# Chunked attention with a top-128 feed-forward: keys in runs of 16 tokens, V without zero blocks, casts off GpSimd, ranks summed on TensorE, a fixed issue order

## The chip, the cores and the metric

The kernel runs on one core of a Trainium2 chip. The core has five engines with a queue each: TensorE (PE in the profile, with its weight loads as PEld), VectorE (DVE), ScalarE (ACT), GpSimd (POOL) and SyncE (SP, which here only issues transfers). The metric is the device time of one execution in microseconds; the time before is the median of three runs, 202.14 us.

## The reference

The first half is attention in chunks. There are 4 batches, 8 heads, 768 tokens and 64 dimensions a head. Each chunk of 32 queries sees 8 memory keys, up to 16 tokens to the left of the chunk, the chunk itself and up to 8 tokens to its right:

```python
for c in range(nc):
    c_start, c_end = c * 32, c * 32 + 32
    l_start, r_end = max(0, c_start - 16), min(S, c_end + 8)
    k_full = concatenate([mem_k, k[:, :, l_start:r_end]]);  v_full = likewise
    scores = matmul(q_c, k_full.T) / 8
    a = softmax(scores)
    out[:, :, c_start:c_end] = matmul(a, v_full)
```

The second half takes the result as x of 4 x 768 rows of 512 columns and sends the best 128 rows of each batch through a feed-forward:

```python
scores = x @ w_gate
out = x.copy()
for b in range(B):
    top_idx = the 128 rows of batch b with the highest scores
    ye = maximum(x[b, top_idx] @ w1, 0) @ w2          # 512 -> 1024 -> 512
    out[b, top_idx] = x[b, top_idx] + sigmoid(scores)[:, None] * ye
```

## The kernel before

**Attention by pairs of heads.** Two heads form a pair (n), and a batch has four, so there are 16 pairs. Inside a pair, partitions 0 to 63 belong to the first head and 64 to 127 to the second. Three chunks form a group of 96 queries, and a pair has eight groups. A group's three chunks share one window of 120 tokens, which together with the 8 memory keys makes 128 keys. They are stored as 64 partitions with two tokens each: token 2i and 2i+1 lie on partition i (index s is the token's parity), and the memory keys sit on partitions 60 to 63. A mask per partition and chunk (`maskb`) blanks the keys that a chunk does not see; it is the bias of the exponential.

**What is done for a pair.** `tr_q` and `tr_k` transpose queries and keys on TensorE, 16 transposes of 96x64 each, both into the same PSUM tile (tag `tp`, one buffer). ScalarE copies the queries out (L205); VectorE copies the keys out with three copies (L217 for the six inner groups, L219 and L221 for the first and last) into `kw`, which holds the 128 keys of each group; GpSimd adds the memory keys (L223). `cast_v` turns V to 16 bits on GpSimd, two casts of 64 partitions (L230), into `vbd`, which is block diagonal: each head's 64 values and a column of ones have their own columns, and the other head's columns are zero, written once at the start (L160, L161). `scores(u)` does half a pair (u runs over 32 halves): 32 matmuls of 64x64 by 96 columns (L245) into two PSUM banks and three exponentials of 256 elements (L251). `values(u)` does 12 matmuls of 128 partitions by 130 columns, six on 96 queries (L266) and six on 32 (L270), and on VectorE a reciprocal and a product (L274, L275) that write the finished half into `x`.

**Loading.** q and k come through GpSimd's queue and are cast to 16 bits on the way (L77). V comes through SP's queue as 32 bits, in `load_v`: for each head one transfer for the inner groups (L86, 180 KB), one each for the first and last group (L88, L90) and one for the memory values (L93). `load_batch(b+1)` is coded at the second half of batch b; the V tiles have two buffers, and so have the tiles of q and k.

**The feed-forward of a batch** is spread over the eight halves of the next batch by `moe_steps`: `m_store` writes x out through SP (L288, L289), `m_scores` takes the dot products with w_gate on VectorE (L298) and casts x to 16 bits on GpSimd (L300), `m_rows` spreads the scores over all partitions (transposes L308, copies L310), `m_rank` counts for every row how many rows score higher, with a compare that also sums (L325), `m_select` turns the counts into 128 slots, `m_gather` collects the rows by matmul with the one-hot matrix `sel`, `m_ffn1` and `m_ffn2` are the two layers, and the end is a scattered transfer that adds to `out` (L379). Every PSUM tile of this part is the one bank `pm`. The batch that comes last has nothing beside it. The x tiles have two buffers, and transfers to `out` wait for one another where they overlap: the store of a batch and the scatters before and after it.

**The order.** The loop at L409 gives the order in the code, but the framework's planner reorders the instructions of each engine by its own estimates and by when their inputs are due. It decides where the steps of the feed-forward stand among the attention of the next batch.

Of the kernel before, what the change touches and what calls it, by code (L numbers as in the profile page):

```python
# [26 lines left out]
def kernel(  # L27
# [24 lines left out]
    HD = S * D  # L52
    SLOTS = 4
# [3 lines left out]
    att = ctx.enter_context(tc.tile_pool(name="att", bufs=3))  # L57
# [4 lines left out]
    pxx = ctx.enter_context(tc.tile_pool(name="pxx", bufs=2, space=bass.MemoryType.PSUM))  # L62
    ptt = ctx.enter_context(tc.tile_pool(name="ptt", bufs=1, space=bass.MemoryType.PSUM))
    pmm = ctx.enter_context(tc.tile_pool(name="pmm", bufs=1, space=bass.MemoryType.PSUM))


    q16s, k16s, v32s = {}, {}, {}
    vbufs = [cst.tile([128, NP, NG, 128], FP, tag=f"v32_{i}", name=f"v32_{i}") for i in range(2)]

    def alloc_batch(b):  # L70
        q16s[b] = ld.tile([96, H, 512], F16, tag="q16", name=f"q16_{b}")
        k16s[b] = ld.tile([96, H, 512], F16, tag="k16", name=f"k16_{b}")
        v32s[b] = vbufs[b % 2]
# [6 lines left out]
    def load_v(b, p0, n):  # L80
        t = v32s[b]
        for h in range(2):
            base = (b * H + 2 * p0 + h) * HD
            o = 64 * h
            for i in range(n):
                nc.sync.dma_start(out=t[o:o + 60, p0 + i, 1:7, :],  # L86
                                  in_=_dap(v, base + 2 * i * HD + 80 * D, [[2 * D, 60], [96 * D, 6], [1, 128]]))
            nc.sync.dma_start(out=t[o + 8:o + 60, p0:p0 + n, 0, :],  # L88
                              in_=_dap(v, base, [[2 * D, 52], [2 * HD, n], [1, 128]]))
            nc.sync.dma_start(out=t[o:o + 56, p0:p0 + n, 7, :],  # L90
                              in_=_dap(v, base + 656 * D, [[2 * D, 56], [2 * HD, n], [1, 128]]))
            for i in range(n):
                nc.sync.dma_start(out=t[o + 60:o + 64, p0 + i, :, :],  # L93
                                  in_=_dap(mem_v, (b * H + 2 * (p0 + i) + h) * n_mem * D,
                                           [[2 * D, 4], [0, NG], [1, 128]]))


    memk16 = cst.tile([n_mem, B * H, D], F16, tag="memk16")
    nc.gpsimd.dma_start(out=memk16, in_=_dap(mem_k, 0, [[D, n_mem], [n_mem * D, B * H], [1, D]]))
    alloc_batch(0)  # L100
    load_qk(0, q, q16s[0], 0, 1)
    load_qk(0, k, k16s[0], 0, 1)

    ident = cst.tile([128, 128], FP, tag="ident")
    make_identity(nc, ident)
    ident16 = cst.tile([128, 128], F16, tag="ident16")
    nc.vector.tensor_copy(out=ident16, in_=ident)

# [3 lines left out]
    load_v(0, 0, 1)  # L112
    load_qk(0, q, q16s[0], 1, 1)
    load_qk(0, k, k16s[0], 1, 1)
    load_v(0, 1, 1)
    load_qk(0, q, q16s[0], 2, 2)
    load_qk(0, k, k16s[0], 2, 2)
    load_v(0, 2, 2)

    wgb = cst.tile([128, Dm], FP, tag="wgb")  # L120
    nc.sync.dma_start(out=wgb, in_=_dap(moe_w_gate, 0, [[0, 128], [1, Dm]]))
    w1_sb = cst.tile([128, 4, F], F16, tag="w1")
    w2_sb = cst.tile([128, 8, Dm], F16, tag="w2")

# [5 lines left out]
    kp = cst.tile([128, 1], FP, tag="kp")  # L130
    for h in range(2):
        nc.gpsimd.iota(kp[64 * h:64 * h + 64, :], pattern=[[0, 1]], base=0, channel_multiplier=1,
                       allow_small_or_imprecise_dtypes=True)
    ismem = cst.tile([128, 1], FP, tag="ismem")
    nc.vector.tensor_scalar(out=ismem, in0=kp, scalar1=59.5, scalar2=None, op0=ALU.is_gt)
    maskb = cst.tile([128, 3], FP, tag="maskb")
    tmpm = cst.tile([128, 3], FP, tag="tmpm")
    for c in range(3):
        nc.vector.tensor_scalar(out=maskb[:, c:c + 1], in0=kp, scalar1=16.0 * c - 0.5, scalar2=None, op0=ALU.is_gt)
        nc.vector.tensor_scalar(out=tmpm[:, c:c + 1], in0=kp, scalar1=16.0 * c + 27.5, scalar2=None, op0=ALU.is_lt)  # L140
    nc.vector.tensor_tensor(out=maskb, in0=maskb, in1=tmpm, op=ALU.mult)
    nc.vector.tensor_tensor(out=maskb, in0=maskb, in1=ismem.to_broadcast([128, 3]), op=ALU.add)
    nc.vector.tensor_scalar(out=maskb, in0=maskb, scalar1=1.0, scalar2=-MASKED, op0=ALU.subtract, op1=ALU.mult)


    ones8 = cst.tile([128, NG], F16, tag="ones8")
    nc.vector.memset(ones8, 1.0)
    nc.vector.tensor_scalar(out=ones8[:, 0:1], in0=kp, scalar1=7.5, scalar2=None, op0=ALU.is_gt)
    nc.vector.tensor_scalar(out=tmpm[:, 0:1], in0=kp, scalar1=55.5, scalar2=None, op0=ALU.is_lt)
    nc.vector.tensor_tensor(out=ones8[:, 7:8], in0=tmpm[:, 0:1], in1=ismem, op=ALU.add)  # L150

    vbds, kws = [], []
    for i in range(SLOTS):
        vb = cst.tile([128, NG, 2, 130], F16, tag=f"vbd{i}", name=f"vbd{i}")
        kw = cst.tile([128, NG, 128], F16, tag=f"kw{i}", name=f"kw{i}")
        vbds.append(vb)
        kws.append(kw)
        nc.vector.memset(kw[:, 0, 0:16], 0.0)
        nc.vector.memset(kw[:, 7, 112:120], 0.0)
        nc.gpsimd.memset(vb[0:64, :, :, 65:130], 0.0)  # L160
        nc.gpsimd.memset(vb[64:128, :, :, 0:65], 0.0)  # L161
        for h in range(2):
            o = 64 * h
            nc.vector.tensor_copy(out=vb[o:o + 64, :, :, 65 * h + 64],
                                  in_=ones8[o:o + 64, :].unsqueeze(2).to_broadcast([64, NG, 2]))


    p_mk = ptt.tile([128, B * NP, n_mem], F16, tag="tp", name="p_mk")
    for pr in range(B * NP):
        nc.tensor.transpose(out=p_mk[:, pr, :], in_=memk16[:, 2 * pr:2 * pr + 2, :],  # L170
                            identity=ident16[0:n_mem, 0:n_mem])
    memkT = cst.tile([128, B * NP, n_mem], F16, tag="memkT")
    nc.vector.tensor_copy(out=memkT, in_=p_mk)


    iota1 = cst.tile([128, cap], F16, tag="iota1")
    nc.gpsimd.iota(iota1, pattern=[[1, cap]], base=1, channel_multiplier=0, allow_small_or_imprecise_dtypes=True)
    ltri = cst.tile([128, 128], F16, tag="ltri")
    nc.gpsimd.memset(ltri, 1.0)
    nc.gpsimd.affine_select(out=ltri, in_=ltri, pattern=[[1, 128]], compare_op=ALU.is_gt, fill=0.0,  # L180
                            base=0, channel_multiplier=-1)
    ones6 = cst.tile([128, NB], FP, tag="ones6")
    nc.vector.memset(ones6, 1.0)
    auxs = []
    for i in range(2):
        a = cst.tile([128, NB, 3], F16, tag=f"aux{i}", name=f"aux{i}")
        nc.gpsimd.iota(a[0:96, :, 0], pattern=[[96, NB]], base=0, channel_multiplier=1,
                       allow_small_or_imprecise_dtypes=True)
        nc.gpsimd.iota(a[96:128, :, 0], pattern=[[32, NB]], base=576, channel_multiplier=1,
                       allow_small_or_imprecise_dtypes=True)  # L190
        auxs.append(a)


    qTs = {}

# [204 lines left out]


    NPR = B * NP
    NU = 2 * NPR
    tr_q(0)
    tr_k(0)
    cast_v(0)
# [58 lines left out]
```

The softmax here doesn't subtract the row's maximum and nothing guards it: scores larger than these inputs give would overflow.

## Time and profile before

| | |
|---|---|
| median of 3 runs | 202.14 us (200.54 to 204.42) |
| the profiled execution | 200.01 us, its span 198.6 us |
| granted TensorE clock, mean over the span | 0.747 |
| busiest engines | PE 125.2 us, DVE 117.0 us, POOL 83.4 us |
| transfers | 24.49 MB in 29561 packets |
| V transfers issued by SP | 100 |
| last L275 of batches 1, 2 and 3 | 86, 126 and 168 us |

The profile's times run from the first instruction. L12 is line 12 of the kernel. A busy share is an average over stages that are limited by different things. An issue row of SP (SPq) gives the time in which SP handed out a transfer, not the time of the transfer. A windows row gives the busy time of each engine in that stretch with the number of instructions, then the granted clock (1.00 is full speed), the share of the 16 transfer engines that was busy, and GB/s.

### The profile page before, as it was taken

To read this page: it belongs to the slowest core of one execution; us is meant where nothing else is said; L and a number is where in the kernel's file an instruction comes from. 1 tells how busy PE (TensorE), PEld (TensorE's weight loads), DVE (VectorE), ACT (ScalarE), POOL (GpSimd) and SP (SyncE) were. 2 spreads that over 40 slices of the span, in tenths; PEclk is the share of its full clock that TensorE was granted. 3 is DMA by queue.
4 is the path that set the end of the run, shared out by engine and by line. 5 is a ranking of instruction groups with operands and counts; after the bars stand their busy time and mean duration, and the time that the engine had idled before them with its cause. 6 is when DMAs were issued, how large, how long until landed. Compare 5 with 4: busy or idle time off the path is not lost. (4 is left out here: it accounts for less than half of the span.)

```text
span 198.6 us, 4328 instructions
## 1 busy us (share of the span) xinstructions
PE 125.2 (63%) x1732; PEld 94.8 (48%) x1732; DVE 117.0 (59%) x309; ACT 62.6 (32%) x137; POOL 83.4 (42%) x104
## 2 busy tenths in 40 slices
PE   0313794958975499973685999567256994306550
PEld 0202673746645277842563787345155772105510
DVE  4284354342899921798998024999950459894010
ACT  2101552418544122654062317232102570200200
POOL 7999993034998000467404040679300004500020
PEclk9999998585995555896579559955558799555885
DMA  5997899999799999603987600049100000364003
GB/s 77 214 208 163 186 189 215 217 210 209 125 251 282 216 211 211 143 4 53 262 196 158 122 0 3 0 56 272 45 0 3 0 3 0 36 192 143 0 0 53
DMA packets 29561, 24.49 MB, mean 123 GB/s; under 512 B 2150, under 2 KB 25318, under 8 KB 29542
## 3 DMA queue, kind: packets, MB, share of 16 engines
q1 hardware_dynamic: 20438, 14.75, 30.1%
q0 software_dynamic: 9104, 9.47, 29.8%
q8 instruction: 13, 0.21, 0.5%
q14 instruction: 6, 0.05, 0.1%
HBM read 25.30 MB, written 7.34 MB: 164 GB/s over the span
## 5 line engine op out<-in xcount | busy, mean ns | idle before, releaser
L251 ACT ACTIVATE es<-p_s,maskb 128x256 f16<-128x256 f32 x96 | 37.8, 476 | 34.2 <-PE p_s L245 31.1
L230 POOL CAST vbd<-v 64x1024 f16<-64x1024 f32 x32 | 35.5, 1158 | 12.8 <-DMA v<-in_mem_v_dram 10.8
L300 POOL CAST x<-x 128x1536 f16<-128x1536 f32 x8 | 13.6, 1705 | 41.1 <-DVE x L275 41.1
L298 DVE SCALAR_TENSOR_TENSOR junk<-x,wgb 128x512 f32<-128x512 f32 x24 | 30.6, 1301 | 0.1
L245 PE MATMUL p_s<-qT,kw 64*64 64x96 f16 x512 | 23.9, 247 | 4.5 <-DVE kw L219 2.5
L217 DVE COPY kw<-p_tk 128x720 f16<-128x720 f16 x16 | 14.4, 902 | 19.2 <-PE p_tk L213 19.2
L245 PEld LDWEIGHTS <-kw 64*64 64x64 f16 x512 | 18.3, 137 | 12.5 <-issue 4.7
L325 DVE TENSOR_SCALAR_CACHE_REDUCE jr<-brow,scr 128x768 f16<-128x768 f32 x24 | 23.0, 1001 | 1.2 <-ACT brow L310 1.2
L205 ACT COPY qT<-p_tq 128x768 f16<-128x768 f16 x16 | 12.8, 803 | 33.3 <-PE p_tq L201 33.3
L201 PE MATMUL p_tq<-ident,q 96*64 96x96 f16 x256 | 14.2, 250 | 14.0 <-DVE kw L221 12.1
L266 PE MATMUL p_x<-vbd,es 128*96 128x130 f16 x192 | 21.2, 259 | 2.3 <-ACT es L251 0.9
L274 DVE RECIPROCAL rd<-p_x 128x6 f32<-128x6 f32 x32 | 6.0, 191 | 27.1 <-PE p_x L270 26.5
L270 PE MATMUL p_x<-vbd,es 128*32 128x130 f16 x192 | 19.9, 248 | 0.0
L266 PEld LDWEIGHTS <-es 128*96 128x96 f16 x192 | 16.4, 149 | 6.1 <-ACT es L251 2.4
L223 POOL COPY kw<-memkT 128x64 f16<-128x64 f16 x16 | 5.0, 317 | 32.9 <-PE p_s L245 32.4
L201 PEld LDWEIGHTS <-q 96*64 96x64 f16 x256 | 9.7, 135 | 17.5 <-issue 12.3
L275 DVE TENSOR_TENSOR x<-p_x,rd 128x384 f32<-128x384 f32 x32 | 17.5, 551 | 0.6
L308 PE MATMUL p_b<-ident,scr 128*128 128x128 f32 x24 | 8.2, 376 | 13.2 <-DVE junk L298 9.9
L213 PE MATMUL p_tk<-ident,k 96*64 96x96 f16 x256 | 12.9, 254 | 5.4 <-ACT qT L205 4.4
L270 PEld LDWEIGHTS <-es 128*32 128x32 f16 x192 | 12.9, 107 | 6.4 <-issue 3.0
L379 POOL DMA_INDIRECT out_dram<-y,idx x4 | 6.7, 1670 | 21.0 <-DVE y L378 20.5
L348 PE MATMUL p_e<-sel,x 128*128 128x128 f16 x96 | 13.3, 304 | 1.9 <-DVE sel L340 1.9
(70 smaller groups left out, 140.0 us busy)
## 6 DMA issues: line engine op xcount, KB each, us to landing
v<-in_v_dram SPq DMA_DIRECT2D x32, 180.0 KB
out_dram<-x SPq DMA_DIRECT2D x4, 1152.0 KB
q<-in_q_dram POOLq DMA_DIRECT2D x7, 384.0 KB, 9.6
k<-in_k_dram POOLq DMA_DIRECT2D x7, 384.0 KB, 11.8
w_sb<-in_moe_w_dram POOLq DMA_DIRECT2D x2, 1024.0 KB, 20.6
out_dram<-x SPq DMA_DIRECT2D x4, 384.0 KB
v<-in_v_dram SPq DMA_DIRECT2D x14, 56.0 KB
v<-in_v_dram SPq DMA_DIRECT2D x14, 52.0 KB
```

Of the source, the lines that this page charges most:

```text
L201: nc.tensor.transpose(out=p_t[64 * h:64 * h + 64, j, :], in_=q16s[b][:, 2 * pr + h, 64 * j:64 * j + 64], identity=ident16[0:96, 0:96])
L217: nc.vector.tensor_copy(out=kw[:, 1:7, 0:120].rearrange("p g (t j) -> p g t j", j=8), in_=_sap(p_t, 10, [[12, 6], [1, 15], [96, 8]]))
L230: nc.gpsimd.tensor_copy(out=vb[o:o + 64, :, :, 65 * h:65 * h + 64], in_=v32s[b][o:o + 64, pr, :, :].rearrange("p g (s d) -> p g s d", d=D))
L245: nc.tensor.matmul(out=p_s[o:o + 64, s, 96 * gi:96 * gi + 96], lhsT=kw[o:o + 64, g, s:128:2], rhs=qf[o:o + 64, 96 * g:96 * g + 96], start= ...
L251: nc.scalar.activation(out=es[:, :, :, 32 * c:32 * c + 32], in_=pv[:, :, :, 32 * c:32 * c + 32], func=AF.Exp, bias=maskb[:, c:c + 1], scal ...
L266: nc.tensor.matmul(out=p_x[0:96, gi, :], lhsT=es[:, s, gi, :], rhs=vb[:, GROUPS[half][gi], s, :], start=(s == 0), stop=(s == 1))
L270: nc.tensor.matmul(out=p_x[96:128, c, :], lhsT=es[:, s, 3, 32 * c:32 * c + 32], rhs=vb[:, GROUPS[half][3], s, :], start=(s == 0), stop=(s ...
L275: nc.vector.tensor_tensor(out=xs[b][:, 3 * half:3 * half + 3, 128 * pr:128 * pr + 128].rearrange("p g (h d) -> p g h d", d=D), in0=pv[:, : ...
L298: nc.vector.scalar_tensor_tensor(out=junk, in0=x[:, bl, :], scalar=1.0, in1=wgb, op0=ALU.mult, op1=ALU.mult, accum_out=m.scr[:, bl:bl + 1])
L300: nc.gpsimd.tensor_copy(out=m.x16[:, lo:hi, :], in_=x[:, lo:hi, :])
L325: nc.vector.tensor_scalar(out=jr, in0=m.brow, scalar1=m.scr[:, bl:bl + 1], scalar2=None, op0=ALU.is_gt, op1=ALU.add, accum_out=m.cnt[:, bl ...
L348: nc.tensor.matmul(out=p_e[:, dch, :], lhsT=m.x16[:, bl, 128 * dch:128 * dch + 128], rhs=m.sel[:, bl, :], start=(bl == 0), stop=(bl == NB ...
```

## The change

- V is loaded so that a partition holds a run: token t of a group's window goes to partition 16 j + i with t = 8 i + 2 j + s, so each head has four blocks (j) of 15 partitions, and the memory values sit on the 16th partition of each block. `load_v` issues each transfer once for each block.
- The keys follow the same order: two copies (one for each s) of 512 elements with 16 in a row, out of a transpose tile with zero columns at both ends, so that the first and last group need no copies of their own. GpSimd then writes the memory keys over the 16th column of each run.
- V has no zero blocks: `vc` has 65 columns a head. `values` does 24 matmuls a half of 64 partitions by 65 columns, each head into its own PSUM bank; `normalise` handles a whole pair with one reciprocal and one product. `p_x` has one buffer of two banks in place of two of one.
- The cast of V moves to ScalarE (one of 128 partitions), the cast of x to VectorE.
- The rank: `m_cmp` only writes 0 or 1, and `m_count` sums them on TensorE, 36 matmuls of one column, and one that clears the bank.
- The issue order is the order of the code on every engine (`manual_schedule`). The loop goes by pairs, with 24 steps of the feed-forward on six hooks of each pair. Scores run one pair ahead, keys and V casts two, queries three. V of batch b+2 is asked for at pair 2 of batch b.
- In the last batch the feed-forward uses the two-buffer scores tile in PSUM, and 384 of the 512 columns of its dot products and casts are done before the last pair.
- At the start, fewer constants are made ahead of the first pair; V of batch 0 comes pair by pair, and all of q and k of batch 0 is asked for at once.

```diff
-    att = ctx.enter_context(tc.tile_pool(name="att", bufs=3))
+    att = ctx.enter_context(tc.tile_pool(name="att", bufs=4))
-    pxx = ctx.enter_context(tc.tile_pool(name="pxx", bufs=2, space=bass.MemoryType.PSUM))
+    pxx = ctx.enter_context(tc.tile_pool(name="pxx", bufs=1, space=bass.MemoryType.PSUM))
+    ctx.enter_context(tc.manual_schedule())
...
     def load_v(b, p0, n):
         for h in range(2):
+            for jj in range(4):
+                o = 64 * h + 16 * jj
+                base = (b * H + 2 * p0 + h) * HD + 2 * jj * D
+                for i in range(n):
+                    nc.sync.dma_start(out=t[o:o + 15, p0 + i, 1:7, :],
+                                      in_=_dap(v, base + 2 * i * HD + 80 * D, [[8 * D, 15], [96 * D, 6], [1, 128]]))
+                nc.sync.dma_start(out=t[o + 2:o + 15, p0:p0 + n, 0, :],
+                                  in_=_dap(v, base, [[8 * D, 13], [2 * HD, n], [1, 128]]))
+                nc.sync.dma_start(out=t[o:o + 14, p0:p0 + n, 7, :],
+                                  in_=_dap(v, base + 656 * D, [[8 * D, 14], [2 * HD, n], [1, 128]]))
             for i in range(n):
-                nc.sync.dma_start(out=t[o:o + 60, p0 + i, 1:7, :],
...
-            nc.sync.dma_start(out=t[o + 8:o + 60, p0:p0 + n, 0, :],
...
-            nc.sync.dma_start(out=t[o:o + 56, p0:p0 + n, 7, :],
...
-                nc.sync.dma_start(out=t[o + 60:o + 64, p0 + i, :, :],
+                nc.sync.dma_start(out=t[64 * h + 15:64 * h + 64:16, p0 + i, :, :],
...
+    for p0 in range(NP):
+        load_v(0, p0, 1)
...
     def tr_k(n):
+        for s in range(2):
+            nc.vector.tensor_copy(out=kw[:, :, s, :].rearrange("p g (j t) -> p g j t", t=16),
+                                  in_=_sap(p_t, 100 * s, [[12, NG], [200, 4], [1, 16]]))
+    def mem_k(n):
+        nc.gpsimd.tensor_copy(out=kw.rearrange("p g s (j t) -> p g (s j) t", t=16)[:, :, :, 15],
...
     def cast_v(n):
-        for h in range(2):
-            nc.gpsimd.tensor_copy(out=vb[o:o + 64, :, :, 65 * h:65 * h + 64],
...
+        nc.scalar.copy(out=vcs[n % SLOTS][:, :, :, 0:64],
+                       in_=vbufs[b % 2][:, pr, :, :].rearrange("p g (s d) -> p g s d", d=D))
...
+    def values(n, half):
+        for r0, r1, gis in ((0, 96, (0, 1, 2)), (96, 128, (3, 3, 3))):
+            for i, gi in enumerate(gis):
+                c0 = 65 * (3 * half + i)
+                q0, q1 = (0, 96) if gi < 3 else (32 * i, 32 * i + 32)
+                for s in range(2):
+                    for h in range(2):
+                        o = 64 * h
+                        nc.tensor.matmul(out=p_x[r0:r1, h, c0:c0 + 65], lhsT=es[o:o + 64, s, gi, q0:q1],
+                                         rhs=vc[o:o + 64, GROUPS[half][gi], s, :], start=(s == 0), stop=(s == 1))
+    def normalise(n):
+        nc.vector.reciprocal(out=rd, in_=pv[:, :, :, 64:65])
+        nc.vector.tensor_tensor(
+            out=xs[b][:, :, 128 * pr:128 * pr + 128].rearrange("p g (h d) -> p h g d", d=D),
+            in0=pv[:, :, :, 0:64], in1=rd.to_broadcast([128, 2, NB, D]), op=ALU.mult)
...
+    def m_bank(b, shape, dt=FP):
+        if b == LAST:
+            t = pss.tile([128, 2, 512], FP, tag="ps", name="p_l")
+            return t
+        return pmm.tile([128, 1, 512], FP, tag="pm", name="p_m")
+    def m_x16(b, lo, hi, c0=0, c1=Dm):
+        nc.vector.tensor_copy(out=mods[b].x16[:, lo:hi, c0:c1], in_=xs[b][:, lo:hi, c0:c1])
+    def m_cmp(b, bls):
+        for bl in bls:
+            nc.vector.tensor_scalar(out=m.gr[:, bl, :], in0=m.brow, scalar1=m.scr[:, bl:bl + 1], scalar2=None,
+                                    op0=ALU.is_lt)
+    def m_count(b, bls):
+        if 0 in bls:
+            nc.tensor.matmul(out=m.p_c[:, 0, 0:NB], lhsT=ltri, rhs=zero6, start=True, stop=False, skip_group_check=True)
+        for bl in bls:
+            for ic in range(NB):
+                nc.tensor.matmul(out=m.p_c[:, 0, ic:ic + 1], lhsT=m.gr[:, bl, 128 * ic:128 * ic + 128], rhs=onec,
+                                 start=False, stop=(bl == NB - 1), skip_group_check=True)
...
     def moe_steps(b):
+            [lambda: m_alloc(b), lambda: m_dot(b, (0,))],
+            [lambda: m_dot(b, (1,))],
+            [lambda: m_dot(b, (2, 3))],
+            [lambda: m_dot(b, (4,))],
+            [lambda: m_dot(b, (5,))],
+            [lambda: m_row(b, 0, 4), lambda: m_x16(b, 0, 2)],
+            [lambda: m_row(b, 4, 6), lambda: m_x16(b, 2, 4)],
+            [lambda: m_gate(b)],
+            [lambda: m_cmp(b, (0, 1))],
+            [lambda: m_cmp(b, (2,))],
+            [lambda: m_cmp(b, (3, 4))],
+            [lambda: m_cmp(b, (5,)), lambda: m_x16(b, 4, 6)],
+            [lambda: m_count(b, range(0, 3))],
+            [lambda: m_count(b, range(3, 6)), lambda: m_mask(b)],
+            [],
+            [lambda: m_select(b)],
+            [],
             [lambda: m_gather(b)],
+            [lambda: m_aux(b)],
             [lambda: m_ffn1(b, 0)],
+            [],
             [lambda: m_ffn1(b, 1)],
+            [],
             [lambda: m_ffn2(b)],
...
+    for n in range(NPR):
+        if b >= 1 and pr == 0:
+            m_store(b - 1)
+        scores(n + 1, 0)
+        hook(0)
+        tr_k(n + 2)
+        mem_k(n + 2)
+        hook(1)
+        values(n, 0)
+        cast_v(n + 2)
+        hook(2)
+        scores(n + 1, 1)
+        hook(3)
+        tr_q(n + 3)
+        hook(4)
+        values(n, 1)
+        normalise(n)
+        hook(5)
+        if pr == 2 and b + 2 < B:
+            alloc_batch(b + 2)
+            for p0 in (0, 2):
+                load_qk(b + 2, q, q16s[b + 2], p0, 2)
+                load_qk(b + 2, k, k16s[b + 2], p0, 2)
+                load_v(b + 2, p0, 2)
+        if n == NPR - 2:
+            m_alloc(LAST)
+            m_dot(LAST, range(NB), 0, 384, scrA)
+            m_x16(LAST, 0, NB, 0, 384)
+    b = LAST
+    m_store(b)
+    m_dot(b, range(NB), 384, 512, scrB)
+    nc.vector.tensor_tensor(out=mods[b].scr, in0=scrA, in1=scrB, op=ALU.add)
+    m_row(b, 0, 4)
+    m_row(b, 4, 6, "dve")
+    m_cmp(b, range(NB))
+    m_count(b, range(NB))
+    m_gate(b)
+    m_x16(b, 0, NB, 384, 512)
+    m_mask(b)
+    m_select(b)
+    m_gather(b)
+    m_aux(b)
+    m_ffn1(b, 0)
+    m_ffn1(b, 1)
+    m_ffn2(b)
```

## The prediction

> **What bounds the kernel now.** First the page's busy shares, clock and DMA row.
>
> ```profile
> span 198.6 us, 4328 instructions
> ...
> PE 125.2 (63%) x1732; PEld 94.8 (48%) x1732; DVE 117.0 (59%) x309; ACT 62.6 (32%) x137; POOL 83.4 (42%) x104
> ...
> PEclk9999998585995555896579559955558799555885
> DMA  5997899999799999603987600049100000364003
> ```
>
> No engine is full. The transfers are, for the first 16 slices (80 us); after that the DMA row has holes and the clock sits at half speed in many slices. So I cut the span by stage, at the ends of batches 1 and 2 (the last L275 of a batch), and read the windows.
>
> ```profile
> 0.00:50.00 50.00, 27.10 (x464) 22.20 (x464) 21.64 (x71) 17.24 (x35) 34.04 (x55) 0.87 1.02 189
> 86.00:126.00 40.00, 31.07 (x455) 23.48 (x455) 26.27 (x63) 15.35 (x35) 14.66 (x15) 0.74 0.43 99
> ```
>
> The columns are PE, PEld, DVE, ACT, POOL busy, clock, DMA share, GB/s. Batch 0 waits for data (DMA share 1.02). Batch 2 takes 40 us, 10 a pair, with PE at 31.1 and DVE at 26.3: neither full, so handovers between the two fill the rest. The groups say what makes DVE late.
>
> ```profile
> L230 POOL CAST vbd<-v 64x1024 f16<-64x1024 f32 x32 | 35.5, 1158 | 12.8 <-DMA v<-in_mem_v_dram 10.8
> L298 DVE SCALAR_TENSOR_TENSOR junk<-x,wgb 128x512 f32<-128x512 f32 x24 | 30.6, 1301 | 0.1
> L217 DVE COPY kw<-p_tk 128x720 f16<-128x720 f16 x16 | 14.4, 902 | 19.2 <-PE p_tk L213 19.2
> L325 DVE TENSOR_SCALAR_CACHE_REDUCE jr<-brow,scr 128x768 f16<-128x768 f32 x24 | 23.0, 1001 | 1.2 <-ACT brow L310 1.2
> L266 PE MATMUL p_x<-vbd,es 128*96 128x130 f16 x192 | 21.2, 259 | 2.3 <-ACT es L251 0.9
> ```
>
> L298 averages 1301 ns, but takes 670 to 690 in the timeline where POOL is idle and up to 3.5 us where POOL casts (at 129.36 beside L230): the casts on POOL cost DVE some 24 x 0.62 = 15 us. Last, the queue that the change loads most: SP's timeline.
>
> ```profile
> 2.76 0.34 SPq L86 DMA_DIRECT2D v<-in_v_dram  x1
> 3.13 0.42 SPq L88 DMA_DIRECT2D v<-in_v_dram  x1
> 3.60 0.37 SPq L90 DMA_DIRECT2D v<-in_v_dram  x1
> 4.02 0.31 SPq L93 DMA_DIRECT2D v<-in_mem_v_dram  x1
> ...
> 80.57 0.82 SPq L86 DMA_DIRECT2D v<-in_v_dram  x2
> 81.43 0.42 SPq L88 DMA_DIRECT2D v<-in_v_dram  x1
> 81.90 0.38 SPq L90 DMA_DIRECT2D v<-in_v_dram  x1
> 82.33 0.66 SPq L93 DMA_DIRECT2D v<-in_mem_v_dram  x2
> ```
>
> Where SP waits for nothing, the next issue begins 0.35 to 0.47 us later: four in 1.61 us at the start (4.37 - 2.76), six in 2.46 later. The 180 KB L86 and the two after it take longest; the 16 KB L93 takes 0.31 to 0.35.
>
> **Step 1, V through SP.** Keys in runs of 16 tokens split each L86, L88, L90 into four of 15, 13 or 14 partitions. load_v(b, p, 1) goes from 8 issues to 26, a load of two pairs from 12 to 36: V0 4 x 26 = 104, V1 to V3 72 each, 320 against 100. Price of one, from both sides: 0.35 (L93's period) to 0.47 (L88's). The split leaves the rows and bytes alike, so I let only the excess over 0.35 be shared out: (1.61 - 4 x 0.35) / 13 = 0.016 and (2.46 - 6 x 0.35) / 18 = 0.02: **0.37 us**, nearest to L93's row. SP's order is V0, w_gate, V1, V2 (coded at pair 2), the store of batch 0, V3 (pair 6), the store of batch 1. A pair's V lands 2.5 us after its last issue (estimate; q and k take 6 to 12 under load). V0 starts at 0.8, so pairs 0 to 3 land at 13, 22.5, 32 and 41.5, where the old kernel had pair 3 cast by 30.5; V1's halves at 39.7 + 13.3 + 2.5 = 55.5 and 69, V2's issues end at 93, the store takes 7 (6.78 in the chain) and SP about as long, V3's end at 127, the second store at 134. The x pool has two buffers: pair 12's normalise waits for that second store, as pair 8's does for the first (100).
>
> The Trainium skill's page "DMA: Bandwidth & Descriptors" (Rules for kernel authors) speaks against such a split: transfers under 64 KB pay mostly overhead. Its fit for transfers issued by GpSimd (Anatomy of one DMA), 2.0 us plus bytes at 436 GB/s, would give an estimated 2.1 us for 45 KB, 672 us for 320 in a row; no row shows them in a row, since SP issues the next after 0.4 us.
>
> **Step 2, the start.** The order fixed by hand puts cast_v(n+2) into ACT's queue in iteration n, behind three exps and ahead of three more and the q copy; PE's next key transposes wait for that q copy. So a late V pair stops ACT, then PE: iteration n ends about 3 us after pair n+2 lands (1.07 cast, 1.20 for three exps at L251, 0.80 for the copy). Ends: 35, 44.5, 58.5, then pair 3 at 65 and pair 4 at 72 (69 + 3). The old kernel had pair 4 normalised at 57.4: the start loses some 15 us, though the POOL memsets (7.7 us, L160 and L161) and their DVE stall before 17 us go.
>
> **Step 3, one pair in batches 1 to 3.** By engine:
> - ACT: exps 2 x 1.20, q copy 0.80, the V cast 1.07 (from L205's 803 ns for 768 elements and brow's 0.82 ns an element), MoE 3.0 a batch: 5.0 a pair.
> - DVE: key copies go from 902 + 281 + 256 to two of 512 elements; the rows give 1.06 ns an element, so 0.68 each, 1.36 (half that at best). Normalise: one reciprocal of 0.20 and one of 768 at 0.95 for 2 x (0.19 + 0.55). Dots 6 x 0.75 with POOL quiet. x16's cast comes over from POOL (1.5 us per 1536 there): 3072 elements, 1.6 to 3.3 a batch, I take 2.5. Compares: 0.5 (a write of half the passes) to 1.0 (L325), six a batch, I take 0.75. The rest 4.5 (L340, L378, gate, mask). 2.5 + (4.5 + 2.5 + 4.5 + 4.5) / 4 = 6.5 a pair.
> - PE: 32 transposes and 32 score matmuls as before (16 in 0.46 at full clock, 0.78 at half): 2.5 at the middle. Values: 24 matmuls of 65 columns for 12 of 130 per half. Nearest rows: L245, 0.029 to 0.049 each, gives 0.7 to 1.2 a half; L266's overhead (0.08 and 0.135 each, less 65 columns) gives 1.2 to 1.85. I take 1.2, 2.4 a pair, against 0.93 to 1.58 a half now. The rank adds 37 matmuls at L354's 0.05, 1.9 a batch. Gather, ffn and rows take 6.5 to 12 by clock (16 of L368 in 0.98 or 1.80): 2.8 a pair with the rank, at the middle. Sum 7.7.
>
> PE is longest; with 0.5 for handovers **c = 8.2 us** a pair. Bounds: 6.5 (DVE's sum) and 10 (the pace of batch 2 now). Handovers that are new: p_x has one buffer of two banks, so values(n+1) waits for normalise(n), 1.15 us, covered by scores and key transposes (0.9 to 1.6) as long as DVE has no backlog; mem_k now follows the key copies on POOL (0.24), a whole iteration ahead of its scores, unless POOL sits behind the scatter of a batch that waits for that batch's store.
>
> The same skill's "VectorE: DVE Perf Modes" (The perf-mode tier table) would let one-source fp32 copies and compares in SBUF run two elements a cycle, an estimated 0.55 for a compare; L325 does not show it, since it also accumulates. By that DVE would be at 6 a pair and c still PE's.
>
> Pairs 5 to 14 at 8.2 from 72 end at 154; pair 12 at 138 clears the second store at 134. Pair 15 has no next scores: 7.5, **161.5**.
>
> **Step 4, the tail.** Now 24.1 us from the last L275 (167.9) to y's end (192.1). The last batch's dots over 384 columns run ahead on DVE after pair 14; left are 6 short dots 1.3, add 0.2, rows 1.5, six compares without their accumulator 4.5, count, mask, scan and offset 1.3, first sel 0.2, gather 3.1, copy 0.65, aux 0.3, ffn1 with two PSUM buffers 3.3 (4 now), ffn2 2.5, y 0.8: 19.7. After y, 6.5 to the span's end as now (scatter and landing).
>
> **Sum.** 161.5 + 19.7 + 6.5 = 187.7 span; the profiled execution took 200.01 with a span of 198.6, so add 1.4: 189. That execution lies 1% under the median of 202.14; the same 1% gives **190 us**, 6% below. About 2% is what a measurement of this kernel can tell from no change.
>
> **Rivals.**
> - *SP's issues become the bound (slower).* If a small issue costs what L86 and L88 cost now, the store before pair 12 ends at 15.2 + 320 r (0.8 start, 0.4 w_gate, 7 of SP's time for store 0, 7 for store 1). At r = 0.45 that is 159, pair 15 at 160 + 24, span 210, median 214. It decides from r = 0.38 on (138 = 15.2 + 320 r) and costs over 2% from about 0.43. For: L88's 0.42 to 0.47 and SP's 27 us of waits on earlier V transfers. Against: L93's 0.31.
> - *The fixed order paces like the planner's (slower).* c = 10: 72 + 100 + 9 + 27.6 = 209, median 211. For: in-order queues, the clock at 0.74. Against: 15 us of contention leave DVE.
> - *The matmuls on half the rows save nothing,* 24 at L266's 0.08: 1.9 a half, c = 9.6, 205, median 207. That the unblocked V does not do what it says.
> - *Light issues and a full clock (faster still).* r = 0.35, c = 7: the store lets pair 12 go at 128, three more pairs take 20.5, time 176, median 178.
>
> **How the numbers follow.** Forecast (183 to 197) 0.46; faster still 0.14; between, with r near 0.41 or c near 9 (198 to 206), 0.15; SP bound 0.12; slow order or matmuls 0.13. Faster by 2% (below 198): 0.46 + 0.14 and 0.01 of the cases between, 0.61; same 0.14; slower 0.25. The range takes in the rival at 178 and reaches 210, leaving out the far end of the dear cases.
>
> **What the next profile would show.** SP issues of V every 0.35 to 0.39 us, 104 before 40 us; L298's successor near 0.7 us with no cast on POOL; DVE's normalise of pair 12 waiting for no store; PE's granted clock above 0.75; from 72 us on a pair each 8 us; from the last normalise to y about 20 us. Wrong if SP's V issues reach past 130 us, or if an iteration ends on ACT's cast waiting for V after pair 6.

## The result and the profile after

The changed kernel takes 241.74 us (median; 240.27 to 242.5) against 202.63 us for the kernel before on the same chip. The ratio is 1.196, with a 95% interval of 1.184 to 1.209: **20% slower**, where the prediction said 6% faster. The profiled execution took 242.47 us, of which the span is 240.8.

The page of the changed kernel: span, busy shares, granted clock, DMA row, and the chain that ended last, by engine and by line.

```profile
span 240.8 us, 5533 instructions
...
PE 119.7 (50%) x2264; PEld 98.8 (41%) x2264; DVE 83.8 (35%) x255; ACT 75.3 (31%) x152; POOL 30.7 (13%) x55
...
PEclk9999999999999999999955975557985556677587
DMA  6979994111379222221992275422218380004703
...
SPq 39%; DMA 28%; DVE 10%; PE 9%; issue 9%; ACT 2%; POOL 1%; POOLq 1%; DVEq 0%; ACTq 0%
DMA v<-in_v_dram 22%; SPq L91 16%; SPq L95 9%; SPq L93 8%; SPq L98 6%; DMA out_dram<-x 6%; DVE junk L319 3%; PE p_m L415 3%; DVE gr L353 2%; PE p_x L276 2%; PE p_m L424 2%; ACT es L255 1%; PE p_s L250 1%; PE p_t L203 1%; DVE x L284 1%
```

The computing got lighter, as intended: DVE went from 117.0 us of work to 83.8, POOL from 83.4 to 30.7, and PE from 125.2 to 119.7 at a higher clock (0.837 for 0.747). Yet no engine is busy for more than half of the span, and the DMA row has holes from the seventh slice on (36 us) where it was full to 80 us before. The chain names the holder: 39% of the span is SP issuing, at V's lines L91, L93, L95 and L98, and 22% are V's transfers. From 78 to 114 us, where SP issues V almost without a pause, the DMA row stands at 1 to 2 tenths, so the transfers themselves have room there.

The groups of the changed kernel (page, part 5) show who pays. The last columns are idle time of the engine just before the group and what ended most of it.

```profile
L234 ACT CAST vc<-v 128x1024 f16<-128x1024 f32 x16 | 16.9, 1056 | 86.7 <-DMA v<-in_v_dram 65.3
L220 DVE COPY kw<-p_t 128x512 f16<-128x512 f16 x32 | 12.1, 419 | 74.9 <-PE p_t L203 74.9
...
L284 DVE TENSOR_TENSOR x<-p_x,rd 128x768 f32<-128x768 f32 x16 | 15.3, 958 | 14.6 <-DMA out_dram<-x 14.1
L428 POOL DMA_INDIRECT out_dram<-y,idx x4 | 6.7, 1682 | 75.2 <-DMA out_dram<-x 36.7
L319 DVE SCALAR_TENSOR_TENSOR junk<-x,wgb 128x512 f32<-128x512 f32 (+2 forms) x30 | 15.8, 581 | 0.1
```

ACT stands 86.7 us ahead of its casts of V. The dots of 512 columns among L319 now take 687 ns (1301 before; the row's 581 is a mean with narrower ones), and the key copies 419 ns: these edits did what they should. Normalise L284 also waits 14.1 us for the stores of x, and the scatters on POOL stand behind the same stores.

SP's timeline of the changed kernel, at the start of V2 (start, us, line, instruction, how many):

```profile
99.36 0.86 SPq L91 DMA_DIRECT2D v<-in_v_dram  x2
100.27 0.37 SPq L93 DMA_DIRECT2D v<-in_v_dram  x1
100.69 0.36 SPq L95 DMA_DIRECT2D v<-in_v_dram  x1
101.10 0.84 SPq L91 DMA_DIRECT2D v<-in_v_dram  x2
101.98 0.38 SPq L93 DMA_DIRECT2D v<-in_v_dram  x1
102.41 0.37 SPq L95 DMA_DIRECT2D v<-in_v_dram  x1
...
105.84 1.24 SPq L95 DMA_DIRECT2D v<-in_v_dram  x1
107.12 1.13 SPq L98 DMA_DIRECT2D v<-in_mem_v_dram  x2
```

With no wait in sight the next issue begins 0.41 to 0.44 us after the last, for 45 KB (L91) as for 13 or 14 KB (L93, L95), and the memory values now take 0.56 each. V0 runs to 60 us, V1 to 99, V2 to 139, the store of batch 0 follows, V3 runs from 140.7 to 179.8, then comes the store of batch 1. That is 320 issues in 179 us, **0.56 us each** with all that lies between.

### The profile page after: what moved, and what is told of

Its sections match the earlier page's. It is cut to its first block, busy times and chain, and to the rows that moved or that the text cites. A ratio compares the mean times of both kernels' runs of the same rounds, so it can differ in the third digit from the quotient of the medians.

```text
span 240.8 us, 5533 instructions
## 1 busy us (share of the span) xinstructions
PE 119.7 (50%) x2264; PEld 98.8 (41%) x2264; DVE 83.8 (35%) x255; ACT 75.3 (31%) x152; POOL 30.7 (13%) x55
## 4 chain that ended last, share of the span: by engine, by line
SPq 39%; DMA 28%; DVE 10%; PE 9%; issue 9%; ACT 2%; POOL 1%; POOLq 1%; DVEq 0%; ACTq 0%
DMA v<-in_v_dram 22%; SPq L91 16%; SPq L95 9%; SPq L93 8%; SPq L98 6%; DMA out_dram<-x 6%; DVE junk L319 3%; PE p_m L415 3%; DVE gr L353 2%; PE p_x L276 2%; PE p_m L424 2%; ACT es L255 1%; PE p_s L250 1%; PE p_t L203 1%; DVE x L284 1%
## 5 line engine op out<-in xcount | busy, mean ns | idle before, releaser
L234 ACT CAST vc<-v 128x1024 f16<-128x1024 f32 x16 | 16.9, 1056 | 86.7 <-DMA v<-in_v_dram 65.3
L220 DVE COPY kw<-p_t 128x512 f16<-128x512 f16 x32 | 12.1, 419 | 74.9 <-PE p_t L203 74.9
L276 PE MATMUL p_x<-vc,es 64*96 64x65 f16 (+1 forms) x768 | 33.4, 242 | 0.0
L203 PE MATMUL p_t<-ident,k 96*64 96x96 f16 x256 | 12.7, 267 | 35.3 <-ACT qT L211 35.3
L276 PEld LDWEIGHTS <-es 64*96 64x96 f16 (+1 forms) x768 | 26.5, 142 | 5.2 <-issue 0.6
L203 PEld LDWEIGHTS <-k 96*64 96x64 f16 x256 | 10.5, 152 | 37.1 <-issue 36.3
L227 POOL COPY kw<-memkT 128x64 f16<-128x64 f16 x16 | 9.0, 564 | 128.0 <-DVE kw L220 88.5
L284 DVE TENSOR_TENSOR x<-p_x,rd 128x768 f32<-128x768 f32 x16 | 15.3, 958 | 14.6 <-DMA out_dram<-x 14.1
L319 DVE SCALAR_TENSOR_TENSOR junk<-x,wgb 128x512 f32<-128x512 f32 (+2 forms) x30 | 15.8, 581 | 0.1
L211 ACT COPY qT<-p_t 128x768 f16<-128x768 f16 x16 | 12.9, 809 | 2.7 <-PE p_t L203 2.7
L353 DVE TENSOR_SCALAR gr<-brow,scr 128x768 f16<-128x768 f32 x24 | 13.4, 617 | 0.1
L203 PE MATMUL p_t<-ident,q 96*64 96x96 f16 x256 | 12.3, 263 | 1.9 <-DVE kw L220 1.8
```

Of the source, the lines that this page charges most:

```text
L203: nc.tensor.transpose(out=p_t[64 * h:64 * h + 64, j, 2:98], in_=src[b][:, 2 * pr + h, 64 * j:64 * j + 64], identity=ident16[0:96, 0:96])
L234: nc.scalar.copy(out=vcs[n % SLOTS][:, :, :, 0:64], in_=vbufs[b % 2][:, pr, :, :].rearrange("p g (s d) -> p g s d", d=D))
L276: nc.tensor.matmul(out=p_x[r0:r1, h, c0:c0 + 65], lhsT=es[o:o + 64, s, gi, q0:q1], rhs=vc[o:o + 64, GROUPS[half][gi], s, :], start=(s == 0 ...
L284: nc.vector.tensor_tensor(out=xs[b][:, :, 128 * pr:128 * pr + 128].rearrange("p g (h d) -> p h g d", d=D), in0=pv[:, :, :, 0:64], in1=rd.t ...
L319: nc.vector.scalar_tensor_tensor(out=junk[:, c0:c1], in0=x[:, bl, c0:c1], scalar=1.0, in1=wgb[:, c0:c1], op0=ALU.mult, op1=ALU.mult, accum ...
L353: nc.vector.tensor_scalar(out=m.gr[:, bl, :], in0=m.brow, scalar1=m.scr[:, bl:bl + 1], scalar2=None, op0=ALU.is_lt)
```

## The experiments

Theory 1: the number of V's issues on SP sets the end. Its rivals are the pace of the fixed order and the new matmuls, the stores queued behind V, and the transfers themselves.

### Undo one part: the keys' order, and with it V's split

Keys and values go back to runs of 4 tokens, so that V needs 104 issues; all else stays as changed.

```diff
-            for jj in range(4):
...
+                nc.sync.dma_start(out=t[o:o + 60, p0 + i, 1:7, :], ...)
+            nc.sync.dma_start(out=t[o + 8:o + 60, p0:p0 + n, 0, :], ...)
+            nc.sync.dma_start(out=t[o:o + 56, p0:p0 + n, 7, :], ...)
...
-            out=kw[:, :, s, :].rearrange("p g (j t) -> p g j t", t=16)
+            out=kw[:, :, s, 0:60].rearrange("p g (t j) -> p g t j", j=4)
```

(the places of the memory keys and values and the mask constants follow)

> The changed kernel with one part undone: keys and values stand in the order of the kernel before (runs of 4 tokens, token pairs in one row of partitions), so V needs 104 issues on SP in place of 320; everything else of the change stays. Theory 1 (the number of V's issues on SP sets the end: 320 at some 0.54 us each with their waits): V0 is issued by about 20 us and V3 before 120 us, ACT's casts wait for V only in batch 0, and pairs follow every 6 to 7 us: 165 us (155 to 178), faster than both kernels. Rival (the order fixed by hand, the single p_x buffer or the 64-row matmuls pace the kernel, V only follows them): the time stays above 215 us. Key copies should grow from 0.42 to about 0.5 to 0.6 us each, which is 0.3 us a pair.

**177.82 us, ratio 0.895 (0.888 to 0.902)**: at the upper end of theory 1's range, and 10% faster than the kernel before. ACT's wait ahead of the casts falls from 86.7 to 22.1 us, by 64.6; the span falls from 240.8 to 176.0, by 64.8. SP issues its last V at 93 us. Two details of the expectation were missed: V0 was issued by 27 us and not 20, and ACT still waited 11.5 us for V of pair 4, the first pair of batch 1. The windows of this variant between the ends of normalise of pairs 3, 7 and 11 (columns: PE, PEld, DVE, ACT, POOL busy, clock, DMA share, GB/s):

```profile
63.00:90.90 27.90, 27.17 (x537) 22.56 (x534) 20.93 (x53) 18.27 (x38) 2.90 (x5) 1.00 0.93 207
90.90:119.10 28.20, 24.57 (x564) 20.20 (x563) 21.11 (x54) 18.62 (x38) 4.07 (x5) 0.82 0.37 90
```

Batch 2 takes 28.2 us, 7.05 a pair, where the kernel before took 40. The rival that the order and the half-row matmuls pace the kernel falls. The key copies take 0.65 us (a little over the 0.5 to 0.6 expected): runs of 16 save 0.46 us of DVE a pair, and that is what the 216 additional issues (320 for 104) bought.

### Add one part to the kernel before: V cut in four

```diff
-                nc.sync.dma_start(out=t[o:o + 60, p0 + i, 1:7, :], ...)
+                for a in range(0, 60, 15):
+                    nc.sync.dma_start(out=t[o + a:o + a + 15, p0 + i, 1:7, :], ...)
```

(and the edges in quarters of 13 and 14)

> The kernel before with one thing added: every V transfer cut into quarters of 13, 14 or 15 partitions, the same bytes to the same places, so 292 V issues on SP in place of 76, and with the 32 of the memory values unchanged 324 or so. Theory 1 (issues on SP are the bound): 0.42 to 0.55 us each puts the last V of batch 3 at 150 to 185 us, and the kernel goes from 202 to 225 to 245 us. Rival (the extra issues are hidden, the loss lies in the other parts of the change): 200 to 207 us.

The count in this expectation is off: the kernel has 272 issues of V for 68, with the 32 of the memory values 304 for 100. **240.27 us, ratio 1.209 (1.195 to 1.222)**: the split alone, with the same bytes to the same places and nothing else of the change, costs all of the loss. SP's timeline of this kernel, the last quarter of V2:

```profile
123.56 3.52 SPq L87 DMA_DIRECT2D v<-in_v_dram  x8
127.12 1.63 SPq L91 DMA_DIRECT2D v<-in_v_dram  x4
128.80 1.66 SPq L94 DMA_DIRECT2D v<-in_v_dram  x4
130.50 0.65 SPq L97 DMA_DIRECT2D v<-in_mem_v_dram  x2
```

Again 0.42 to 0.45 us an issue. The memory values, to four neighbouring partitions here, take 0.33 (x2 in 0.65).

### Half of V0 from another engine

```diff
         for h in range(2):
+            eng = nc.scalar if b == 0 and h == 1 else nc.sync
...
```

(the four `dma_start` of `load_v` then go to `eng`)

> The changed kernel with the issues of the odd heads of batch 0 moved from SP to ACT: 52 of V0's 104 issues on each queue, all later ones on SP as before. Theory 1 (SP's issuing is the bound from the first transfer on): V0 is issued by some 32 us in place of 60, all that follows on SP comes some 25 us earlier, time 210 to 222 us. Rival (in the first 60 us the transfers themselves, or a limit on how many are under way, are the bound, and the issuing engine is not): 233 to 242 us, V0's last pair still landing past 50 us.

**225.89 us, ratio 1.134 (1.125 to 1.143)**, between the two expectations and nearer to theory 1. V0's issues end at 35 us in place of 60, V3's at 163.8 in place of 179.8. The start of ACT's own work in this kernel's timeline shows the price:

```profile
34.74 0.56 ACTq L99 DMA_DIRECT2D v<-in_mem_v_dram  x1
35.39 1.28 ACT L212 ACT_TABLE_LOAD   x1 [35.39 <-DMA v<-in_v_dram]
```

Most issues take ACT 0.31 to 0.4 us, as they take SP, and ACT computes nothing until all its 52 are out: pair 0 is normalised at 50 us, not 31, and of the 25 us 16 are left by the end of V3's issues. Here the page "Trainium Kernel Development and Optimization" of the Trainium skill (Key Constraints) bears on the run: transfers issued by different engines share the same DMA engines, and several issuers save only the sequencer's issue time. The run agrees, with the point that this "only" was worth 25 us of V0 here. It also rules out a limit on the transfers under way as the bound of V0: the trace's records show that SP and ACT shared eight semaphores here, four each, where SP had used all eight alone (the last section says more), so no more transfers could be under way than before.

### The stores off SP

```diff
-        nc.sync.dma_start(out=_dap(out, b * S * Dm, ...), in_=x[0:96, :, :])
+        nc.gpsimd.dma_start(out=_dap(out, b * S * Dm, ...), in_=x[0:96, :, :])
```

(and the second store likewise)

> The changed kernel with the stores of x issued by GpSimd in place of SP, so that they no longer queue behind V3 (and V1's successors) on SP. Theory 1 (V's issues are the bound, the stores behind them cost what normalise waits for them, 14 us, of which V's own pace takes most back): 228 to 238 us. Rival (the stores queued behind V are the main cause): 205 to 218 us.

**242.45 us, ratio 1.221 (1.210 to 1.232)**: no gain at all, slower than both expectations. Normalise no longer waits for stores (0.6 us idle before it, for 14.6), and V takes it all back: ACT waits 96.9 us ahead of its casts of V in place of 86.7, and V's issues end at 185 us. So the 14.1 us of waits for stores were a second symptom of the late V, not a cost of their own.

### Sixteen issues fewer

```diff
-            for i in range(n):
-                nc.sync.dma_start(out=t[64 * h + 15:64 * h + 64:16, p0 + i, :, :],
-                                  in_=_dap(mem_v, ..., [[2 * D, 4], [0, NG], [1, 128]]))
+        for i in range(n):     # both heads of the pair in one transfer to 8 partitions
+            nc.sync.dma_start(out=t[15:128:16, p0 + i, :, :],
+                              in_=_dap(mem_v, ..., [[2 * D, 8], [0, NG], [1, 128]]))
```

> The changed kernel (keys in runs of 16) with the memory values of a pair's two heads loaded by one transfer to 8 partitions in place of two to 4 each: 16 issues fewer of 320, the same bytes. Theory 1 (each issue on SP costs time in proportion, here 0.56 us each): four issues fewer a batch, the V stream is 2.2 us a batch or 9 us in all shorter, time 230 to 236 us. Rival (not the number of issues, but the bytes or the number of places they go to): 239 to 243 us.

235.46 us, ratio 1.184 (1.173 to 1.194): 6.3 us below the changed kernel by the medians, of the 9 expected. That is not clear of noise: against the kernel before on its own chip (199.57 us) the ratio fell only from 1.196 to 1.184, some 2.5 us, and the two intervals overlap. In the trace V's issues end at 171.9 us in place of 179.8. The merged issue takes 0.64 us in place of 0.56, which may be part of why 16 issues fewer gave less. This run fits theory 1 but does not show it; the undoing and the adding above do.

### What the other parts of the change are worth

All three start from the variant with 4-token keys (177.82 us), so that V's issues no longer cover them.

The fixed order, left to the planner instead:

```diff
-    ctx.enter_context(tc.manual_schedule())
```

> The variant with 4-token keys without the order fixed by hand: the one line that asks for the manual schedule is left out, so that the planner orders the same instructions. Theory (the fixed order is a gain of its own, pairs every 6.9 us against 10 in the kernel before): 185 to 200 us. Rival (the gain of the variant comes from the casts, the rank and the 64-row matmuls; the order is worth nothing or costs something): 170 to 181 us.

192.54 us, ratio 0.967 (0.929 to 1.005): as the theory had it, the order is worth some 15 us. The planner ends the pairs of batch 2 3.5 us apart, but no pair ends for 32 us ahead of them (85.5 to 117.4) and for 25 us behind them (128.0 to 152.8).

The rank by DVE, with an accumulating compare and no matmuls:

```diff
-            nc.vector.tensor_scalar(out=m.gr[:, bl, :], ..., op0=ALU.is_lt)
+            nc.vector.tensor_scalar(out=jr, ..., op0=ALU.is_gt, op1=ALU.add, accum_out=m.cnt[:, bl:bl + 1])
```

> The variant with 4-token keys, with the rank counted by DVE again (compares that accumulate, no matmuls for the count). Theory (compares without accumulator take 0.61 us against 1.0, 24 of them, 9 us of DVE, of which batches 1 to 3 hide most since DVE is busy 52%; the tail loses 6 x 0.4 and gains the count's 1.9): 178 to 183 us. Rival (DVE's compares are on the path in every batch): 184 to 188 us.

185.22 us, ratio 0.930 (0.924 to 0.935): 7.4 us more, in the rival's range. Its group of compares:

```profile
L354 DVE TENSOR_SCALAR_CACHE_REDUCE jr<-brow,scr 128x768 f16<-128x768 f32 x24 | 22.9, 1005 | 0.1
```

1005 ns for 612. Pair 15 ends 5.5 us later (155.7 for 150.2), so most of the loss lies in the batches, which were thought to hide it; six compares of the tail take 5.6 us for 3.27. In this variant PE waits 13.0 us for normalise (0.7 without the edit): with one p_x buffer, whatever stands ahead of normalise in DVE's queue holds PE's values.

The casts back on GpSimd:

```diff
-        nc.scalar.copy(out=vcs[n % SLOTS][:, :, :, 0:64],
+        nc.gpsimd.tensor_copy(out=vcs[n % SLOTS][:, :, :, 0:64],
-        nc.vector.tensor_copy(out=mods[b].x16[:, lo:hi, c0:c1], ...)
+        nc.gpsimd.tensor_copy(out=mods[b].x16[:, lo:hi, c0:c1], ...)
```

> The variant with 4-token keys, with V's cast and the cast to x16 put back on GpSimd. Theory (casts on GpSimd slow DVE beside them, dots from 0.58 back to 1.0 to 1.3 us, and the V cast waits in GpSimd's queue ahead of the q and k loads): 183 to 195 us. Rival (DVE and GpSimd have room, so the place of the casts does not matter): 174 to 181 us.

181.49 us, ratio 0.917 (0.897 to 0.936), between the two expectations; the intervals overlap, so it can't be told from 177.82. The dots do slow down, in this kernel's groups on DVE:

```profile
L319 DVE SCALAR_TENSOR_TENSOR junk<-x,wgb 128x512 f32<-128x512 f32 (+2 forms) x30 | 27.6, 972 | 0.1
```

972 ns for 583 (means over three widths; those of 512 columns take 1135 for 692), 11.7 us more of DVE's work, but DVE lost the x16 casts (7.8 us) at the same time and had room.

### A better version, and a start that is bound by bytes

With V's issues few, the variant's pairs 2 to 4 wait for data: V of pair 4, the first of batch 1, is cast at 54.3 us, though there are few issues on SP by then. Moving loads of other data behind it was tried three times.

```diff
-    load_w()
...
+        if n == 2:
+            load_w()
```

> The variant with 4-token keys, with the two loads of w1 and w2 (2 MB of f32 each) moved from ahead of the first iteration to iteration 2. In that variant V0's last two pairs land at 38.8 and 54.3 us though SP issued them by 27 us, beside the loads of batch 1, the weights and batch 2. Theory (with V's issues few, batch 0 is bound by the bytes that compete with V0; 4 MB at some 210 GB/s are 19 us): pair 3 ends near 48 us in place of 63, time 160 to 168 us. Rival (V0's last pairs are late for another reason, the limit on SP's transfers under way or the memory values' transfers): 174 to 179 us.

178.19 us, ratio 0.899 (0.885 to 0.913): nothing. The expectation counts pair 4's V among V0; it belongs to V1, which SP issued from 31.7 us on. Nor was its theory tested: the weights were issued at 19.4 us, for 15.1 without the edit.

```diff
+        if n == 1:
+            load_qk(1, q, q16s[1], 2, 2)
+            load_qk(1, k, k16s[1], 2, 2)
+        if n == 3:
+            load_w()
...
-        if pr == 2 and b + 2 < B:
+        if pr == (3 if b == 0 else 2) and b + 2 < B:
```

> As the variant with late weights, and further: the second half of batch 1's q and k is issued in iteration 1, the weights in iteration 3, and batch 2's q, k and V in iteration 3 in place of 2. Theory (bytes that compete with V0): pair 3 ends near 42 us, time 155 to 164 us. Rival (competing bytes are not what makes V0 late): 174 to 179 us. If the loads now come too late for batch 1, pairs 5 or 6 wait for their q and the time is 165 to 172 us.

178.27 us, ratio 0.897 (0.870 to 0.924): nothing again, a clear miss. The trace of this kernel says why: POOL has little else in its queue and runs ahead, so the weights are issued at 25 us and batch 2's first q and k at 27 and 31, all the same. A later line of code is a later issue only if the queue ahead of it waits for something. So GpSimd was given such a wait:

```diff
         cast_v(n + 2)
+        if n in (2, 3):
+            nc.gpsimd.tensor_copy(out=pgate, in_=vcs[(n + 2) % SLOTS][:, 0, 0, 0:1])
+        if n == 2:
+            load_w()
```

(the moved loads of q and k as in the run before this one)

> The variant with late loads, and GpSimd now really held back: a copy of one element from the cast V of pair 4 stands ahead of the loads of the weights, and one of pair 5 ahead of batch 2's loads (without them GpSimd ran ahead and issued these at 25 to 33 us). Theory (the 8.7 MB that compete with V1's first half make pair 4 late, its cast at 55 us): pair 4's V is cast near 38 us, time 160 to 170 us. Rival (the bytes are needed soon after anyway, so that later pairs wait for them): 173 to 180 us, with pairs 6 to 9 later than 8 us apart.

**171.05 us, ratio 0.861 (0.855 to 0.867)**, faster than both kernels, and between the two expectations (160 to 170 and 173 to 180). ACT's casts of pairs 4 and 8 in its timeline:

```profile
37.80 1.05 ACT L235 CAST vc<-v 128x1024 f16<-128x1024 f32 x1 [1.09 <-DMA v<-in_v_dram]
...
68.38 1.05 ACT L235 CAST vc<-v 128x1024 f16<-128x1024 f32 x1 [4.49 <-DMA v<-in_mem_v_dram]
```

Pair 4 is cast at 37.8 for 54.3, 16.5 us earlier, but pair 5 then comes 10.5 us after pair 4, with PE waiting 4.3 us for q, and pairs 7 to 9 come 8.5 to 10 us apart, with the wait of 4.49 us above: the bytes put off are needed now. Pair 15 is normalised 8.8 us earlier. So the rival of this run, that the bytes are needed soon after anyway, holds for about half of the 16.5 us.

## Why the prediction was wrong

**Step 1 failed, in the price of one issue.** It set 0.37 us, from bounds of 0.35 to 0.47, by letting "only the excess over 0.35 be shared out": an issue of a quarter was to cost nearly as little as the lightest row. Measured, a quarter costs what the whole did: 0.41 to 0.44 us, where the prediction's own rows give 0.37, 0.47 and 0.42 for the three that were cut, 0.42 on average. So cutting a transfer saves nothing per issue. With all that lies between, SP paid 0.56 us an issue. Three more terms were not in the sum:
- The memory values keep their bytes, but now go to every sixteenth partition: L98 takes 0.56 us where the same 16 KB to four neighbours took 0.33. The step had read their row as the floor.
- SP waits for earlier transfers, 21.5 us in the changed kernel by its waits on V and the memory values. The prediction named "SP's 27 us of waits" for the rival (in the kernel before, all waits on V and the memory values come to 34.6) and put them at nothing in its own price, without a reason.
- A dozen single issues of 1.0 to 2.1 us where the view names no wait, among them the two right after the store of batch 0 (1.9 and 2.1).

The four largest of the waits that make up the 21.5 us (who waits for what: us in all, times, longest):

```profile
SPq L93 <- DMA v<-in_mem_v_dram: 6.5, 4, 2.1
SPq L91 <- DMA v<-in_v_dram: 4.9, 11, 0.8
SPq L93 <- DMA v<-in_v_dram: 4.8, 5, 2.3
SPq L95 <- DMA v<-in_v_dram: 3.4, 7, 0.8
```

320 x 0.42 is 134 us, the memory values add 32 x 0.14 = 4.5, the waits 21.5, and some 19 of the 179 us are left, some 12 of them for those slow single issues, the rest for w_gate, the store and what is smaller; what makes the issues slow is open. So of the 61 us beyond 320 x 0.37, the plain price is only 16, less than the waits. One term was too dear: the store of batch 0 was to hold SP for 7 us, and its two issues took 1.2. V's last issue was forecast for 127 us and came at 179.8. V0's 104 issues were out at 60 us and not before 40, and normalise of pair 12 did wait for the second store, 8.0 us. The page "DMA: Bandwidth & Descriptors" of the Trainium skill (Rules for kernel authors) had spoken against so small transfers, and the outcome agrees with it; the estimate of 2.1 us for 45 KB by that page's fit is not the price that is paid here, since SP pays 0.42 us and the next one goes out beside it.

**The rival "SP's issues become the bound" was right in what it named as the bound, and its formula came close.** It put the end of the second store at 15.2 + 320 r and pair 15 some 25 us later. The store landed at 187.1, which makes r 0.537 (fitted, so this part is no test); from there it gives 212 for pair 15 (measured 214.8) and, with 26.2 to the end, a span of 238 (measured 240.8). Only its r of 0.45 and its chance of 0.12 were too low. The place where the late issues bite was wrong, though: it is not the second store behind V3 that decides, since the stores off SP gain nothing, but V3 itself, by which pairs 12 to 15 go.

**Step 2** had the mechanism, the in-order cast that stops ACT and then PE, but one pair too many: iteration n follows V of pair n+1, not n+2. From the cast of pair 2 (49.5) to normalise of pair 1 (57.25) it is 7.7 us, and the same 7.7 from the cast of pair 3 to pair 2 and of pair 4 to pair 3, since the exps that normalise needs are queued behind that cast. The ends were set at 35, 44.5, 58.5, 65 and 72; they came at 31.7, 58.2, 70.4, 91.6 and 97.2. In the variant with 4-token keys pair 4 ends at 69.1, near the 72 of the forecast, but that is luck: the forecast had SP's issues as the cause, and there it is the loads that compete with V1 (171.05 us with these held back). "After pair 6" was the sign of a wrong forecast, and ACT's timeline shows it, a wait for V ahead of pair 8's cast in the changed kernel:

```profile
123.59 1.05 ACT L234 CAST vc<-v 128x1024 f16<-128x1024 f32 x1 [12.69 <-DMA v<-in_v_dram]
```

**Step 3** was too dear, on the safe side. The variant with 4-token keys shows c where V does not bind: from pair 3 to pair 13 it is 7.0 us a pair (63.0 to 133.3), not 8.2. A pair of its batch 2 has 5.3 us of DVE (6.5 was set, and 0.46 of the 5.3 belongs to the 4-token copies), 4.65 of ACT (5.0) and 6.1 of PE (7.7), at a clock of 0.82. The terms: key copies 0.42 (0.68, or half at best), compares 0.61 (0.75), dots of 512 columns 0.69 (0.75), normalise 0.96 + 0.23 (0.95 + 0.20), V's cast 1.06 (1.07). Values of batch 2 take 7.06 us, 1.77 a pair (2.4), against 9.4 before (L266 and L270 there, at a clock of 0.74); over all 16 pairs it is 31.9 us against 41.1. The rival that half rows save nothing falls, but the saving is 0.6 us a pair, at clocks that differ. The rival of a slow fixed order falls by the windows. The prediction cited the tier table of "VectorE: DVE Perf Modes" in the Trainium skill for a compare of an estimated 0.55 us: the six compares of the tail take 3.27 us, 0.545 each, and agree; beside other work the mean is 0.61.

One term of step 3 was too cheap: pair 15, set at 7.5 us, takes 11.6 in the variant. The last batch's dots and x16 cast, put ahead of it on DVE, take 4.2 us, the gate of the batch before stands behind them, and PE waits 2.7 us for that and then runs ffn1 at half speed (16 matmuls in 1.89 us for 1.00, at a granted clock of 0.50 for 1.00).

**Step 4** was right: from normalise of pair 15 to y it is 19.0 us in the changed kernel (214.8 to 233.7) and 19.2 in the variant, against the 19.7 predicted.

Put together, the parts that the forecast of 190 us rested on are all there, and were worth more than it said: with V's issues few, 177.8. The one part with a price on SP turned them into 241.7.

## What to carry to other kernels

Count a change's DMA issues by their number on the queue, not by their bytes: here each costs SP some 0.42 us whatever its size, and 0.56 with its waits, and 216 more of them cost 60 us or more (241.7 against 177.8; 0.30 in the ratios), more than all other parts of the change gained. A layout that makes a copy on an engine cheaper (0.46 us a pair) is paid for by whoever has to bring the data into it. When a run shows several waits, take one away before believing it: the waits for the stores went and the time stayed.

## What the runs showed of the hardware that was not expected

**The price of an issue does not depend on its size.** In these traces 13 and 45 KB take SP 0.41 to 0.44 us where nothing waits, and in the kernel before 26 to 56 KB take 0.42 to 0.47 and 180 KB 0.37 to 0.43. It does depend on the target: 16 KB to four partitions side by side 0.33, to four that lie 16 apart 0.56, and 32 KB to eight that lie 16 apart 0.64.

**No more than eight of SP's transfers are under way at once, and it is the program that holds them to eight.** The chain of the variant with 4-token keys at its start (start, us, what):

```profile
6.22 6.40 DMA v<-in_mem_v_dram
12.64 9.54 DMA v<-in_mem_v_dram
22.19 11.60 DMA v<-in_mem_v_dram
33.87 12.74 DMA v<-in_v_dram
```

The transfers that start here are the 12th, 20th, 28th and 36th of SP's queue: each is issued as the one eight before it lands. The trace's records say why. Every transfer raises a semaphore (a counter) when it lands, and SP's issues use eight of them in turn, in the kernel before, in the changed one and in this variant alike; an issue that comes to a semaphore again waits for the transfer that used it last. So the eight are how the framework shares out its semaphores; a limit of the chip was not reached. A transfer that lands late thus holds SP back, and small ones land no sooner: the 16 KB of memory values above take 6.4 to 11.6 us to land beside q, k and the weights, and the 180 KB issued at 7.95, 15.16 and 24.71 us take 7.2, 9.5 and 11.9.
